# Respreading small VectorE work in a one-core retention, routing and two-layer expert kernel: decoding, slot positions, gates and one copy move

## Chip, core and metric

The kernel runs on one core of a Trainium2 chip. The metric is device time in microseconds (us) of one launch. Engines are named as the profile names them: PE is TensorE (its weight loads are PEld), DVE is VectorE, ACT is ScalarE, POOL is GpSimd, SP is the engine that issues most transfers.

## What is computed

The reference, cut to what matters:

```
def reference(q, k, v, moe_*, moe2_*):          # float32
    # 1. retention with decay: 4 batches, 8 heads, 576 positions, 64 wide
    scores = (q @ k.T) / 8
    ret = scores * gamma[h] ** (i - j) * (i >= j)
    x = (ret @ v).transpose(0, 2, 1, 3).reshape(2304, 512)
    # 2. router: 8 experts, top 1, one gate per token
    logits = normed(x) @ normed(expert_emb).T / tau
    e = argmax(logits);  gate = softmax(logits)[e]
    x[t] = gate[t] * (relu(x[t] @ w1[e]) @ w2[e])    # 512 -> 1024 -> 512
    # 3. dense layer on all tokens
    h = x @ w_in                                     # 512 -> 2048
    return elu(h) @ w_out                            # 2048 -> 512
```

## The kernel before

Products are made from float32 values split into a high and a low part (`split_of` on ACT makes the high part `ha`/`hb`, `split_low` on DVE the low part `la`/`lb`). The order of the program on each engine is the order of the Python code: nothing is scheduled by cost, and an engine that waits at one instruction holds back all that stands behind it on the same engine. SP likewise issues transfers in program order, on one queue. There are four stretches.

**Retention, 0 to 107 us.** Ten units (`UNITS`, u = 0 to 9) of up to 256 positions. `scale(u)` copies q into the layout that TensorE transposes (L289) and multiplies k by its decay (L282); unit 0 by DVE, all others by POOL. `transposes`, `scores`, `carried`, `values`, `summed` and `xrows` are TensorE's work of a unit, with ACT or DVE taking each result out of PSUM; the mask multiplication of `scores` (L339, tile `A`) is DVE's. Token tiles 0 to 17 are routed in four groups (0 to 4, 5 to 9, 10 to 12, 13 to 17). The small steps of a group (`expert_steps`, `gate_steps`) are generators that `pump` runs between the large instructions. The group of tiles 10 to 12 is the third one, index 2; its last steps, the gates (L570 to L578), run before the mask multiplication of the last unit, u = 9.

**End of the router, 107 to 124 us.** The last group's experts and gates (`ge`, `gg`), the order of the experts by their load (`go`, `order_steps`: tiles `key`, `gtm`, `pe`, `perm`, `pif`, `cnp`, `pi`, and then `pick`, which makes `idsp`, the row numbers of experts 1 to 7), the row numbers and gates of the first expert (`finish`: `ids0`, `gsl0`), and then the gather of the first expert's rows by POOL (L912), their multiplication by the gates (L921, L923), transposes (`xpose`) and the first products. `gather_expert(1)`, the gather of the second expert's rows, needs `idsp`.

**Experts, 120 to 357 us.** A loop over i = 0 to 64, eight steps for each of the eight experts, in the order that the router found. Step i makes `mm1(i)` (the products of the first layer, tile `h`), `mm2(i - 1)` (those of the second layer, tiles `acc`; its last four need `hl`), takes `h` out as `hh` (ACT) and `hl` (DVE, L976), splits one weight tile, loads the weight tile after next, and runs pieces of two other jobs. The first is decoding: the dense layer's weights arrive as 8-byte words and are rebuilt to float32 on DVE, 32 tiles (`draw` in, `wd` out), four DVE instructions each (L151, L153, L156, L159) and one of ACT (L154); `decode(n)` runs n of the four pieces. The last piece (L159) also has SP issue the load of the tile after next and the store of this one. The second is the table that maps output rows back to tokens (`compact`, then 18 times `compact_part`, at the steps in `WHEN`). At i = 48 (`IOVER`) stands a conditional, `overflow`, whose body is not run with these inputs; behind it the rows `yb` of the expert layer, four transfers of 384 KB (L1168, at i = 49 to 52), are loaded for the dense layer, and their sums (L1179, tiles T3, T2, T1, T4) are made by DVE at i = 54 and 55.

**Dense layer, 357 to 738 us.** TensorE with few gaps; the sums, splits and activations are on DVE, ACT and POOL.

Lines that the change and the steps of the prediction touch: `scale` L274 to L293; the pump behind `xrows` L745; the router's end L863 to L870; `compact` L1011 to L1031; the table of the first steps `WHEN` L1195; the decoding at L1306 to L1309; `sums` L1172.

Of the kernel before, what the change touches and what calls it, by code (L numbers as in the profile page):

```python
# [9 lines left out]
F32 = mybir.dt.float32  # L10
# [74 lines left out]
def tile_kernel(ctx: ExitStack, tc: tile.TileContext, q, k, v, emb, tau, w1, w2, w_in, w_out, const, out):  # L85
# [80 lines left out]
    def decode(n):  # L166
        for _ in range(n):
            next(dsteps, None)
# [105 lines left out]
    def scale(u):  # L274
        if u >= NU:
            return
        c = UNITS[u][1]
        scaled[u] = {nm: a2.tile([P, 2, H, D], F32, tag=nm + "s", name=f"{nm}s{u}") for nm in "qk"}
        eng = vec if u == 0 else pool

        def decayed(nm, s_, g_):
            eng.tensor_tensor(out=scaled[u][nm][:, s_], in0=loaded[u][nm][:, :, s_, :],  # L282
                              in1=C("g" + nm)[:, g_ * H:(g_ + 1) * H].unsqueeze(2).to_broadcast([P, H, D]), op=ALU.mult)

        m = len(slots_of(u))
        if u == NU - 1:
            decayed("q", 0, 4)
        else:
            eng.tensor_copy(out=scaled[u]["q"][:, :m].rearrange("p s h d -> p h s d"), in_=loaded[u]["q"][:, :, :m, :])  # L289
        if u == 0:  # L290
            meanwhile()
        for s_ in slots_of(u):
            decayed("k", s_, 2 * c + s_ if c >= 0 else 4)  # L293

    tT = {}
    copied = {}
# [355 lines left out]
    transposes(0, 1, "k")  # L652
    load(1, "v", copied[0, 1, "k"])
    scores(0, 0)
    pe = ps.tile([P, 2, 512], F32, tag="X", name="pemb")[:, 0, :2 * KD * NE].rearrange("p (b k e) -> p b k e", b=2, k=KD)
    for b, src in enumerate((e1, swap.rearrange("e k j d -> e (k j d)"))):
        for kk in range(KD):
# [4 lines left out]
            nc.scalar.copy(out=rhsx[b][o:o + 64, :, j, D:], in_=pe[o:o + 64, b])  # L662
    summed(0)
    transposes(1, 0, "q")
    load(2, "q", copied[1, 0, "q"])

    NG = len(GROUPS)
# [31 lines left out]
    for u in range(NU):  # L699
        ns = UNITS[u][2]  # L700
        before = UNITS[u - 1][2][1] if u and len(UNITS[u - 1][2]) > 1 else None
        if u == 1:
            load(3, "k")
        carried(u)
        scores(u, 1 if UNITS[u][1] >= 0 else 0)
        transposes(u + 1, 0, "qk" if u else "k")
        if u == 0:
            load(2, "k", copied[1, 0, "k"])
            nc.sync.dma_start(out=ct[:, gcols:], in_=const[:, gcols:CSMALL])
            nc.sync.dma_start(out=big[0][:, 2 * P:], in_=const[:, CSMALL + 2 * P:])  # L710
        else:
            load(u + 2, "v", copied.get((u + 1, 0, "k")))
        if held is not None:
            grouped(held)
        if before is not None:
            xrows(before)
        if u < NU - 1:
            pump(24, 0)
        summed(u + 1)
        scale(u + 2)  # L720
        if u == 0:
            pool.tensor_scalar(out=pre[:, 0, :], in0=C("base"), scalar1=1.0 / P, scalar2=None, op0=ALU.mult)
            pool.tensor_copy(out=lowb, in_=C("lower"))
            pool.tensor_copy(out=parts[:, :, :2], in_=C("id").rearrange("p (n two) -> p n two", two=2))
        if u == 7:
            load_a(0)
            load_b(0)
            load_a(1)
        transposes(u + 1, 1)
        load(u + 3 if u else 2, "q" if u else "v", copied.get((u + 1, 1, "k")))  # L730
        if u == NU - 2:
            decode_load(0)
            decode_load(1)
        values(u)
        load(u + 3, "k" if u else "q", copied[u, "x"])
        if before is not None:
            grouped(before)
        if u == NU - 1:
            while live:
                pump(100, 0)  # L740
        if u + 1 < NU and UNITS[u + 1][1] >= 0:
            scores(u + 1, 0)
        xrows(ns[0])
        held = ns[0]
        if u < NU - 1:  # L745
            pump(24, 0)
        for _ in range(6 if u > 6 else 4):
            if ready:
                slots(*ready.pop(0))
# [115 lines left out]
    begin(pig, 2, NPART)  # L865
    warm(8)
    next(fi)
    next(fi, None)
    for _ in interleave(gg, go):
        pass  # L870
    for _ in finish(pig, 2, NPART, gsl, gsl0):
        pass
# [130 lines left out]
        return lambda: eng.value_load(ap, min_val=0, max_val=top)  # L1003

    gather_expert(0)
    pool.memset(ord_["off"][:, 0:1], 0.0)
    for e in range(NE):
        pool.tensor_tensor(out=ord_["off"][:, e + 1:e + 2], in0=ord_["off"][:, e:e + 1], in1=ord_["cnp"][:, e:e + 1], op=ALU.add)
    pool.tensor_copy(out=offi, in_=ord_["off"][:, :NE])

    def compact():  # L1011

        oe = qp.tile([P, NE], F32, name="oe")
        vec.tensor_tensor(out=ord_["t"], in0=ord_["perm"].rearrange("q p e -> q e p"),
                          in1=ord_["off"][:, :NE].unsqueeze(1).to_broadcast([P, NE, NE]), op=ALU.mult)
        vec.tensor_reduce(out=oe, in_=ord_["t"], axis=AX.X, op=ALU.add)
        t = qp.tile([P, NT, NE], F32, name="po1")
        pos = qp.tile([P, NT], F32, name="pos")
        pool.tensor_tensor(out=oe, in0=oe, in1=C("base"), op=ALU.subtract)
        rf = qp.tile([P, NT], F32, name="rf")  # L1020
        pool.tensor_copy(out=rf, in_=rk)
        pool.tensor_tensor(out=t, in0=oh, in1=oe.unsqueeze(1).to_broadcast([P, NT, NE]), op=ALU.mult)
        vec.tensor_reduce(out=pos, in_=t, axis=AX.X, op=ALU.add)
        pool.tensor_tensor(out=pos, in0=pos, in1=rf, op=ALU.add)
        posi = qp.tile([P, 2, NT], I32, name="posi")
        posf = qp.tile([P, 2, NT], F32, name="posf")
        pool.tensor_copy(out=posi[:, 0, :], in_=pos)
        vec.tensor_scalar(out=posi[:, 1, :], in0=posi[:, 0, :], scalar1=127, scalar2=None, op0=ALU.bitwise_and)
        vec.tensor_scalar(out=posi[:, 0, :], in0=posi[:, 0, :], scalar1=7, scalar2=None, op0=ALU.arith_shift_right)
        pool.tensor_copy(out=posf, in_=posi)  # L1030
        return posf  # L1031

    cparts = {}

    def compact_part(n, posf):
        bt = qp.tile([P, P], BF16, name=f"cb{n}")
        at = qp.tile([P, NPART, NT], BF16, name=f"ca{n}")
        o18 = qp.tile([P, NT], BF16, name=f"co{n}", tag="co", bufs=2)
# [153 lines left out]

    QL = 3 * NQ
    MORE = {*range(1, 9), *range(10, 26, 3)}
    WHEN = [i for i in range(10, 38) if i % 8 in (1, 2, 4, 5, 6)]  # L1195
    slots_a = {"A11": 0, "A12": 1, "A22": 2, "S3": 3}
    slots_s = {"S1": 0, "S2": 1, "S4": 2}
    qra, qrs, qrb, qa, qs, qb = {}, {}, {}, {}, {}, {}
# [48 lines left out]
        low()  # L1247
    load_b(1, nc.scalar)
    load_a(2, nc.scalar)
    split_b(0)  # L1250
    for i in range(NI1 + 1):
        if i == IOVER - 1:
# [13 lines left out]
        if i == 0:  # L1266
            for _ in pick(gslp, gsl):
                pass
            gather_expert(1)
        e, f = divmod(i, 8)  # L1270
        if i < NI1:
            if f == 0 and e:
# [3 lines left out]
            if 3 <= f < 6 and e + 1 < NE:  # L1276
                weighs[e + 1](f - 3)
        if i == 9:
            posf = compact()
        if i in WHEN:  # L1280
            compact_part(WHEN.index(i), posf)
        if i == 41:
            compact_sum()
        if i == 42:
# [20 lines left out]
            low_(0, i - IOVER - 8)  # L1305
        elif i < IOVER - 1:  # L1306
            decode(3 if i in MORE else 2)
        elif IOVER < i < IOVER + 4:
            decode(3)  # L1309
        if i == NI1 - 3:  # L1310
            Sa(0)
        if i == NI1 - 2:
# [200 lines left out]
```

## Time and profile before

| | |
|---|---|
| median of 3 runs | 739.19 us (739.15 to 739.63) |
| the profiled execution's own time | 739.86 us |
| its span, first to last instruction | 738.0 us |
| PE busy | 711.1 us (96%) |
| DVE busy | 586.2 us (79%) |
| ACT busy | 447.5 us (61%) |
| POOL busy | 252.4 us (34%) |
| mean granted TensorE clock | 0.989 |

Busy time is the union of the instructions' records. Matmuls overlap in the pipeline and their ends are modelled, so the wait that a row of TensorE names is a little less than the time lost; where the same step recurs, the distance from one step's first product to the next one's tells the loss.

### The profile page before, as it was taken

How to read it: one execution, taken by the hardware profiler on the slowest of the kernel's cores; microseconds unless marked ns; L12 is line 12 of the kernel's file. 1: busy time of each engine (PE TensorE's matmuls, PEld its weight loads, DVE VectorE, ACT ScalarE, POOL GpSimd, SP SyncE). 2: the span in 40 equal slices, each digit the busy share in tenths (PEclk: the TensorE clock that was granted, in tenths of full speed). 3: DMA queues.
4: the chain of work that ended last, by engine and by line, in shares of the span. 5: the costliest groups of instructions: out<-in, count | busy, mean ns of one | idle time of the engine just before them, and what ended most of it. 6: DMA issues, size and time to landing. Idle time of an engine off the chain costs nothing.

```text
span 738.0 us, 15524 instructions
## 1 busy us (share of the span) xinstructions
PE 711.1 (96%) x5940; PEld 656.2 (89%) x5940; DVE 586.2 (79%) x940; ACT 447.5 (61%) x690; POOL 252.4 (34%) x347
## 2 busy tenths in 40 slices
PE   8999968999999999979999999999999999999996
PEld 6988866999999999979988999989999988989995
DVE  4566777889888898749799999987778997777773
ACT  3443443556656566547677677786665877656562
POOL 3436364127573661001522432264112237211103
PEclk9999998999999999989999999999999999999999
DMA  7777555899999989687434222235222124211012
GB/s 214 227 216 216 155 180 173 285 307 301 333 296 336 317 278 307 224 289 222 126 128 118 97 74 84 58 128 186 61 82 58 59 74 155 86 58 58 29 29 85
DMA packets 101987, 123.79 MB, mean 168 GB/s; under 512 B 12266, under 2 KB 72078, under 8 KB 101910
## 3 DMA queue, kind: packets, MB, share of 16 engines
q1 hardware_dynamic: 97622, 111.71, 48.0%
q0 software_dynamic: 3104, 9.83, 3.7%
q10 hardware_dynamic: 1184, 1.24, 0.6%
q8 instruction: 47, 0.77, 0.4%
q14 instruction: 30, 0.25, 0.1%
HBM read 99.91 MB, written 22.85 MB: 166 GB/s over the span
## 4 chain that ended last, share of the span: by engine, by line
issue 27%; PE 15%; POOL 9%; DVE 4%; ACT 2%; DMA 1%; SPq 0%; POOLq 0%; ACTq 0%
PE o L230 4%; PE X L230 3%; PE h L230 3%; PE Y L230 2%; POOL out_dram L1425 2%; POOL qs L1221 2%; POOL qs L1219 2%; POOL qs L1222 2%; POOL qa L1220 2%; PE acc L993 2%; DMA draw<-in_moe_w_in_dram 1%; PE acc L995 1%; DVE hB L1389 0%; DVE glA L1397 0%; DVE xB L1386 0%
## 5 line engine op out<-in xcount | busy, mean ns | idle before, releaser
L1219 POOL TENSOR_TENSOR qs<-qa 128x256 f32<-128x256 f32 x24 | 23.4, 973 | 250.1 <-DMA qa<-wd 52.5
L230 PE MATMUL h<-xth,ha 128*128 128x332 f32 (+7 forms) x252 | 75.1, 314 | 0.1
L993 PE MATMUL acc<-hh,lb 128*128 128x342 f32 (+7 forms) x256 | 73.8, 304 | 0.5 <-DVE lb L204 0.5
L993 PE MATMUL acc<-hh,hb 128*128 128x342 f32 (+7 forms) x256 | 73.7, 304 | 0.0
L230 PE MATMUL h<-xtl,ha 128*128 128x332 f32 (+7 forms) x252 | 72.9, 305 | 0.0
L1376 ACT ACTIVATE rA<-hA 128x768 f32<-128x768 f32 x24 | 20.4, 848 | 54.1 <-DVE hA L1369 54.1
L995 PE MATMUL acc<-hl,hb 128*128 128x342 f32 (+7 forms) x256 | 47.2, 307 | 5.5 <-DVE hl L976 5.4
L1361 DVE TENSOR_TENSOR u<-Y,m 128x384 f32<-128x384 f32 x48 | 26.6, 554 | 30.3 <-PE Y L230 28.3
L993 PEld LDWEIGHTS acc<-hh,lb 128*128 128x128 f32 x256 | 48.4, 189 | 1.0 <-DVE lb L204 1.0
L230 PEld LDWEIGHTS h<-xth,ha 128*128 128x128 f32 x252 | 48.1, 191 | 0.6 <-issue 0.3
L993 PEld LDWEIGHTS acc<-hh,hb 128*128 128x128 f32 x256 | 48.5, 189 | 0.0
L912 POOL DMA_INDIRECT row<-xd,idsp x21 | 24.3, 1158 | 70.7 <-ACT xth L953 61.9
L230 PEld LDWEIGHTS h<-xtl,ha 128*128 128x128 f32 x252 | 48.1, 191 | 0.0
L204 DVE TENSOR_TENSOR la<-ra,ha 128x1024 fp32r<-128x1024 f32 x32 | 39.3, 1230 | 9.9 <-ACT ha L199 9.8
L230 PE MATMUL h<-xth,la 128*128 128x332 f32 (+7 forms) x252 | 46.1, 305 | 0.0
L995 PEld LDWEIGHTS acc<-hl,hb 128*128 128x128 f32 x256 | 39.4, 190 | 6.2 <-DVE hl L976 6.2
L204 DVE TENSOR_TENSOR lb<-rb,hb 128x1024 fp32r<-128x1024 f32 x32 | 39.4, 1230 | 6.8 <-ACT hb L199 6.4
L1425 POOL DMA_INDIRECT out_dram<-ob,idc x18 | 20.3, 1126 | 68.4 <-ACT ob L1422 65.9
L154 ACT ACTIVATE dsq<-draw 128x512 f32<-128x512 f32 x32 | 21.8, 680 | 34.5 <-DVE db L159 10.5
L975 ACT ACTIVATE hh<-h 128x342 fp32r<-128x342 f32 (+7 forms) x64 | 27.2, 424 | 23.9 <-PE h L230 22.3
L230 PEld LDWEIGHTS h<-xth,la 128*128 128x128 f32 x252 | 39.0, 191 | 0.0
L339 DVE TENSOR_TENSOR A<-sc,ctbig 128x512 f32<-128x512 f32 (+1 forms) x36 | 22.1, 655 | 21.2 <-PE sc L334 21.2
(1690 smaller groups left out, 2328.8 us busy)
## 6 DMA issues: line engine op xcount, KB each, us to landing
ra<-in_moe_w_dram SPq DMA_DIRECT2D x31, 512.0 KB
rb<-in_moe_w_dram SPq DMA_DIRECT2D x31, 512.0 KB
qb<-wd SPq DMA_DIRECT2D x48, 256.0 KB
draw<-in_moe_w_in_dram SPq DMA_DIRECT2D x16, 512.0 KB
draw<-in_moe_w_out_dram SPq DMA_DIRECT2D x16, 512.0 KB
wd<-db SPq DMA_DIRECT2D x32, 256.0 KB
qa<-wd SPq DMA_DIRECT2D x24, 256.0 KB
qa<-wd SPq DMA_DIRECT2D x48, 128.0 KB
```

What stands on the lines that cost most here:

```text
L154: nc.scalar.activation(out=sq, in_=hw.bitcast(F32), func=AF.Square)
L204: nc.vector.tensor_tensor(out=lo, in0=src, in1=hi.bitcast(F32), op=ALU.subtract)
L230: nc.tensor.matmul(o, l, r, start=first and n_ == 0, stop=last and n_ == len(seq) - 1, skip_group_check=True)
L339: vec.tensor_tensor(out=t[:, :, :w], in0=sc[j][:, :, :w], in1=m.unsqueeze(1).to_broadcast([P, 4, w]), op=ALU.mult)
L912: pool.indirect_dma_start(out=t[:m].rearrange("p k w -> p (k w)"), out_offset=None, in_=xd[:, :], in_offset=bass.IndirectOffsetOnAxis(ap=i ...
L975: nc.scalar.activation(out=hh, in_=hp[:, :c], func=AF.Relu)
L993: nc.tensor.matmul(acc[d][:, :c], w[d][w_], hh, start=f == 0 and w_ == 0, stop=False)
L995: nc.tensor.matmul(acc[d][:, :c], w[d][0], hl, start=False, stop=f == 7)
L1219: pool.tensor_tensor(out=S1, in0=A21, in1=A22, op=ALU.add)
L1361: vec.tensor_tensor(out=S_[nm], in0=S_["Y"], in1=S_["m1"], op=ALU.add)
L1376: nc.scalar.activation(out=Q[n]["r" + z], in_=Q[n]["h" + z], func=AF.Relu, scale=-1.0)
L1425: ins = pool.indirect_dma_start(out=out[:, :], out_offset=bass.IndirectOffsetOnAxis(ap=idc[:, col:col + 1], axis=0), in_=ob, in_offset=None)
```

## The change

Five edits:

- **Second q by VectorE.** POOL no longer copies q of unit 1. DVE does, in two halves (`ordered(1, 0)` and `ordered(1, 1)`), each in front of the transposes that read it or well before.
- **Third group's gates.** The pump behind `xrows` in unit 8 runs one step in place of 24, so the gates of group 2 run after the last unit's `values` have been issued.
- **Router's end.** The last group's gates run without the order steps between them. The order steps and `idsp` run behind the first expert's transposes, in front of `split_b(0)`. The eight running sums of `off` (POOL) run behind `gather_expert(1)`.
- **Positions.** `compact` becomes a generator that runs over i = 9, 10 and 11; `WHEN` begins at 12 in place of 10 and ends one step later.
- **Decoding.** Behind the conditional nine pieces run as 3, 2, 0, 2, 2 at i = 49 to 53 in place of 3, 3, 3 at i = 49 to 51.

```
@@ scale
         if u == NU - 1:
             decayed("q", 0, 4)
-        else:
+        elif u != 1:
             eng.tensor_copy(out=scaled[u]["q"][:, :m].rearrange("p s h d -> p h s d"), in_=loaded[u]["q"][:, :, :m, :])
...
+    def ordered(u, s_):
+        vec.tensor_copy(out=scaled[u]["q"][:, s_], in_=loaded[u]["q"][:, :, s_, :])
@@ before the loop over units
     scores(0, 0)
+    ordered(1, 0)
...
     summed(0)
     transposes(1, 0, "q")
+    ordered(1, 1)
@@ loop over units, behind xrows(ns[0])
-            pump(24, 0)
+            pump(1 if u == NU - 2 else 24, 0)
@@ router's end
     next(fi)
+    while next(gg) != STEP:
+        pass
+    next(gg)
     next(fi, None)
-    for _ in interleave(gg, go):
+    for _ in gg:
         pass
@@ behind gather_expert(0): the running sums become a function, offsets(), called behind gather_expert(1)
@@ compact: three yields, the POOL and DVE instructions as before
-        return posf
+        cparts["pos"] = posf
+        yield
@@ tables
-    WHEN = [i for i in range(10, 38) if i % 8 in (1, 2, 4, 5, 6)]
+    REST = {IOVER + 1: 3, IOVER + 2: 2, IOVER + 4: 2, IOVER + 5: 2}
+    WHEN = [i for i in range(12, 39) if i % 8 in (1, 2, 4, 5, 6)]
@@ in front of the loop over i
     load_a(2, nc.scalar)
+    for _ in go:
+        pass
     split_b(0)
@@ in the loop over i
             gather_expert(1)
+            offsets()
...
-            posf = compact()
+            where_ = compact()
+        if 9 <= i < 12:
+            next(where_)
...
-        elif IOVER < i < IOVER + 4:
-            decode(3)
+        elif i in REST:
+            decode(REST[i])
```

How the rows move on DVE, at three places. A name ends in the number of its step, tile or unit and a number of the buffer; line numbers from L289 on are 3 to 17 higher in the changed kernel.

Behind the conditional, DVE, from the second product part of i = 51 on, before:

```order
L976 SCALAR_TENSOR_TENSOR hl51_6044<-h51_6030,hh51_6043 128x282
L204 TENSOR_TENSOR lb26_6061<-rb26_5427,hb26_6060 128x1024
L156 SCALAR_TENSOR_TENSOR db128_6026<-draw28_5377,db128_6026 128x512
L159 SCALAR_TENSOR_TENSOR db128_6026<-dsq28_6025,db128_6026 128x512
L151 TENSOR_SCALAR db129_6082<-draw29_6022 128x512
L976 SCALAR_TENSOR_TENSOR hl52_6098<-h52_6084,hh52_6097 128x282
```

And the same stretch of the changed kernel, up to the sums of `yb` that open the dense layer's operands:

```order
L204 TENSOR_TENSOR lb26_6060<-rb26_5428,hb26_6059 128x1024
L984 SCALAR_TENSOR_TENSOR hl52_6089<-h52_6075,hh52_6088 128x282
L962 TENSOR_TENSOR xtl_7_6105<-tp7_0_6106,xth_7_6104 128x4x128
L204 TENSOR_TENSOR la27_6115<-ra27_5919,ha27_6114 128x1024
L153 SCALAR_TENSOR_TENSOR db128_6027<-draw28_5378,db128_6027 128x512
L156 SCALAR_TENSOR_TENSOR db128_6027<-draw28_5378,db128_6027 128x512
L984 SCALAR_TENSOR_TENSOR hl53_6147<-h53_6133,hh53_6146 128x282
L962 TENSOR_TENSOR xtl_7_6105<-tp7_1_6162,xth_7_6104 128x4x128
L204 TENSOR_TENSOR lb27_6171<-rb27_5967,hb27_6170 128x1024
L159 SCALAR_TENSOR_TENSOR db128_6027<-dsq28_6026,db128_6027 128x512
L151 TENSOR_SCALAR db129_6190<-draw29_6023 128x512
L984 SCALAR_TENSOR_TENSOR hl54_6206<-h54_6192,hh54_6205 128x282
```

The first piece of tile 29 (L151, which reads `draw29`) stood in front of `hl52` and now stands in front of `hl54`. Behind `hl54` both programs have the last transposed part, then `la28`, then the first sum of `yb` (T3, which needs all four transfers). On SP's queue the load of `draw30` and a store of `wd`, which L159 of tile 28 issues, stood in front of the load of `ra29` and the last `yb` transfer, and now stand behind them and the load of `rb29`.

In the last units of the retention, DVE, before (`A00_9` and `A10_9` are the masks of the last unit, `gate2` the third group's gates):

```order
L442 TENSOR_REDUCE lg3_2012<-lh15_2199 128x8
L570 TENSOR_REDUCE gate2_2031<-ex2_2030 128x3
L572 TENSOR_SCALAR gate2_2031<-gate2_2031 128x3
L574 RECIPROCAL gate2_2031<-gate2_2031 128x3
L578 CAST parts_75<-gate2_2031 128x3
L581 TENSOR_TENSOR gate2_2031<-gate2_2031,parts_75 128x3
L339 TENSOR_TENSOR A00_9_2259<-sc0_9_0_2241,ctbig_135 128x4x64
```

And of the changed kernel:

```order
L445 TENSOR_REDUCE lg3_2013<-lh15_2200 128x8
L342 TENSOR_TENSOR A00_9_2252<-sc0_9_0_2234,ctbig_135 128x4x64
L342 TENSOR_TENSOR A10_9_2254<-sc1_9_0_2235,ctbig_135 128x4x64
L442 TENSOR_TENSOR xs16_2263<-xa16_2258,ct_67 128x512
L444 TENSOR_TENSOR lh16_2265<-xa16_2258,ct_67 128x64
L445 TENSOR_REDUCE lg3_2013<-lh16_2265 128x8
L573 TENSOR_REDUCE gate2_2032<-ex2_2031 128x3
```

Eight gate steps (of which the first rows show five) moved from in front of the masks to behind tile 16's results, in front of tile 17's `lg`.

At the router's end, DVE, the place to which the order steps moved, of the changed kernel (before, `lb0` stands directly behind the `xtl` row):

```order
L962 TENSOR_TENSOR xtl_0_2478<-tp0_2_2495,xth_0_2477 128x4x86
L793 SCALAR_TENSOR_TENSOR key_2387<-cn_2386,ct_67 128x8
L795 SCALAR_TENSOR_TENSOR key_2387<-ohf_79,key_2387 128x8
L797 TENSOR_TENSOR gtm_2388<-key_2387 128x64
L799 TENSOR_REDUCE pe_2389<-gtm_2388 128x8
L801 TENSOR_TENSOR perm_2390<-pe_2389,ct_67 128x64
L807 TENSOR_REDUCE cnp_2532<-gtm_2388 128x8
L809 CAST pi_83<-pif_2531 1x8
L818 TENSOR_TENSOR pick_2539<-perm_2390,ids_76 128x192
L822 TENSOR_REDUCE idsp_81<-pick_2539 128x24
L204 TENSOR_TENSOR lb0_2543<-rb0_1927,hb0_2542 128x1024
```

Twelve rows in all moved there (nine are shown); before, they stood one by one between the last group's gate steps.

## Rows read from the trace of the kernel before

**Rows 1.** Page, part 1: busy time, share, instructions.

```profile
PE 711.1 (96%) x5940; PEld 656.2 (89%) x5940; DVE 586.2 (79%) x940; ACT 447.5 (61%) x690; POOL 252.4 (34%) x347
```

**Rows 2.** Windows by TensorE's steps: length, busy of five engines, PEclk, DMA share, GB/s.

```profile
309.78:313.28 3.50, 3.50 (x31) 3.50 (x29) 2.36 (x4) 1.80 (x3) 0.00 (x0) 1.00 0.79 262
313.28:322.88 9.60, 4.68 (x31) 4.43 (x30) 3.13 (x6) 2.45 (x4) 0.00 (x0) 0.82 1.02 359
322.88:328.02 5.14, 5.14 (x30) 4.95 (x28) 2.50 (x4) 2.54 (x4) 0.00 (x0) 0.68 0.85 278
331.28:334.40 3.12, 3.12 (x26) 3.12 (x25) 3.08 (x5) 0.58 (x2) 0.00 (x0) 1.00 0.50 168
```

**Rows 3.** Timeline behind the conditional: start, us, engine, line, operation [idle before, releaser].

```profile
320.23 0.43 DVE L151 TENSOR_SCALAR db<-draw 128x512 int32<-128x512 int32 x1 [6.47 <-DMA draw<-in_moe_w_in_dram]
321.07 1.31 PE L995 MATMUL acc<-hl,hb 128*128 128x282 f32 x4 [4.92 <-DVE hl L976]
323.21 0.51 SPq L1168 DMA_DIRECT2D yb<-yd  x1
...
330.48 0.95 DVE L1179 TENSOR_TENSOR yb<-yb 128x768 f32<-128x768 f32 x1
...
332.34 0.45 DVE L976 SCALAR_TENSOR_TENSOR hl<-h,hh 128x282 fp32r<-128x282 f32 x1
```

**Rows 4.** Two windows of DMA traffic behind the conditional; columns as in rows 2.

```profile
316.00:324.00 8.00, 3.08 (x15) 2.92 (x14) 2.99 (x6) 0.74 (x3) 0.00 (x0) 0.71 1.04 379
325.00:328.00 3.00, 3.00 (x21) 2.83 (x20) 1.59 (x2) 0.81 (x2) 0.00 (x0) 0.80 0.83 263
```

**Rows 5.** Timeline of the first units, q and k of unit 1.

```profile
5.35 0.69 DVE L289 COPY qs<-q 128x1024 f32<-128x1024 f32 x1 [5.35 <-DMA q<-in_q_dram]
...
11.72 1.04 POOL L289 COPY qs<-q 128x1024 f32<-128x1024 f32 x1 [7.55 <-DMA q<-in_q_dram]
13.24 2.04 POOL L282 TENSOR_TENSOR ks<-k,ct 128x512 f32<-128x512 f32 x2 [0.48 <-DMA k<-in_k_dram]
...
12.81 0.66 PE L309 MATMUL qTp<-ident,qs 128*128 128x128 f32 x4 [0.90 <-POOL qs L289]
```

**Rows 6.** Timeline of the last unit of the retention.

```profile
100.62 0.17 DVE L570 TENSOR_REDUCE gate<-ex 128x3 f32<-128x24 f32 x1
...
102.20 0.17 DVE L578 CAST parts<-gate 128x3 bf16<-128x3 f32 x1
...
105.76 0.23 DVE L434 TENSOR_REDUCE lg<-xa 128x8 f32<-128x64 f32 x1 [1.70 <-PE xa L427]
...
102.75 1.02 PE L372 MATMUL xTp<-A,v 64*64 64x64 f32 x32 [0.95 <-DVE A L339]
```

**Rows 7.** Windows of TensorE's steps i = 9 and i = 11; columns as in rows 2.

```profile
153.97:157.60 3.63, 3.63 (x26) 3.63 (x25) 3.50 (x7) 2.39 (x6) 0.00 (x0) 1.00 0.96 300
161.31:166.19 4.88, 4.20 (x26) 3.66 (x25) 4.21 (x8) 0.74 (x2) 3.88 (x7) 1.00 0.85 288
```

**Rows 8.** Timeline of the router's end and the first expert's start.

```profile
111.10 0.13 DVE L788 SCALAR_TENSOR_TENSOR key<-cn,ct 128x8 f32<-128x8 f32 x1
...
114.08 0.35 DVE L817 TENSOR_REDUCE idsp<-pick 128x24 int32<-128x192 f32 x1
...
116.29 0.72 ACT L923 ACTIVATE row<-row,gsl 128x512 f32<-128x512 f32 x1 [4.60 <-DMA row<-xd,ids]
...
117.20 1.44 PE L948 MATMUL tp<-ident,row 128*128 128x128 f32 x8
...
123.31 1.22 DVE L204 TENSOR_TENSOR lb<-rb,hb 128x1024 fp32r<-128x1024 f32 x1 [2.28 <-ACT hb L199]
```

**Rows 9.** Timeline of the second expert's gather, its first issue and first use.

```profile
118.82 1.00 POOL L912 DMA_INDIRECT row<-xd,idsp  x1 [0.40 <-issue]
...
132.69 0.71 ACT L923 ACTIVATE row<-row,gslp 128x512 f32<-128x512 f32 x1
```

**Rows 10.** POOL's `cb` instructions by shape: least/median/most ns, from when to when.

```profile
L1039 POOL TENSOR_SCALAR cb<-ct,posf x18: 595/602/2776, 163.8 to 259.2; 128x128 bf16<-128x128 f32 x18
```

More of the change, by code (lines that the diff above doesn't have):

```diff
@@ L1005, in tile_kernel, with offsets @@
     gather_expert(0)
[L1006 to L1009, printed above, removed]
+    def offsets():
+        off, cnp = ord_["off"], ord_["cnp"]
+        pool.memset(off[:, 0:1], 0.0)
+        for e in range(NE):
+            pool.tensor_tensor(out=off[:, e + 1:e + 2], in0=off[:, e:e + 1], in1=cnp[:, e:e + 1], op=ALU.add)
+        pool.tensor_copy(out=offi, in_=off[:, :NE])
     def compact():
@@ L1018, in compact @@
         pos = qp.tile([P, NT], F32, name="pos")
+        rf = qp.tile([P, NT], F32, name="rf")
+        posi = qp.tile([P, 2, NT], I32, name="posi")
+        posf = qp.tile([P, 2, NT], F32, name="posf")
         pool.tensor_tensor(out=oe, in0=oe, in1=C("base"), op=ALU.subtract)
-        rf = qp.tile([P, NT], F32, name="rf")
         pool.tensor_copy(out=rf, in_=rk)
         pool.tensor_tensor(out=t, in0=oh, in1=oe.unsqueeze(1).to_broadcast([P, NT, NE]), op=ALU.mult)
+        yield
         vec.tensor_reduce(out=pos, in_=t, axis=AX.X, op=ALU.add)
         pool.tensor_tensor(out=pos, in0=pos, in1=rf, op=ALU.add)
-        posi = qp.tile([P, 2, NT], I32, name="posi")
-        posf = qp.tile([P, 2, NT], F32, name="posf")
         pool.tensor_copy(out=posi[:, 0, :], in_=pos)
+        yield
         vec.tensor_scalar(out=posi[:, 1, :], in0=posi[:, 0, :], scalar1=127, scalar2=None, op0=ALU.bitwise_and)
@@ L1030, in compact, with compact_part @@
         pool.tensor_copy(out=posf, in_=posi)
-        return posf
+        cparts["pos"] = posf
+        yield
     cparts = {}
-    def compact_part(n, posf):
+    def compact_part(n):
+        posf = cparts["pos"]
         bt = qp.tile([P, P], BF16, name=f"cb{n}")
@@ L1278, in tile_kernel @@
         if i == 9:
-            posf = compact()
+            where_ = compact()
+        if 9 <= i < 12:
+            next(where_)
         if i in WHEN:
-            compact_part(WHEN.index(i), posf)
+            compact_part(WHEN.index(i))
         if i == 41:
```

## The prediction

> **What bounds it now.** The page's busy times come first: PE works in 96% of the span [rows 1], so an edit can only pay where PE stands still or runs at a lower clock. The list of PE's waits gives the places, and one is far larger than the rest: 4.92 us for `hl` behind the conditional [rows 3]. The chain that ended last is mostly PE's own work and names no other engine for a long piece, so I read the stretches where PE waits, one by one: a timeline of each, and windows cut at the starts of PE's steps, which tell what a step costs beside its neighbours. PE's work is unchanged; whatever brings PE forward at one place carries through to the end, as long as nothing that it meets later becomes late. Each term below is therefore a shift of PE.
>
> **Unit 1's q.** PE's transposes start at 12.81 after a wait for POOL's copy, which began when q landed, at 11.72, and took 1.04; DVE copied a whole q of that size in 0.69 [rows 5]. The half that DVE now copies lies between 0.35 (half of that) and 0.69; I take 0.40, since a fixed part of each instruction doesn't halve. PE starts at 11.72 + 0.40 + 0.03 = 12.15: **0.65 gained** (0.35 to 0.70). The next thing that could be late is POOL's decay of k, whose two halves end at 15.28 [rows 5] and wait for k, not for POOL; half of it is done by 14.26, and PE, earlier by 0.65, uses that half about 14.65. The Trainium skill speaks against this edit: "SBUF — State Buffer", section "Who interferes with whom", says that a VectorE copy can take a port pair that GpSimd needs, as an exclusive lock for a whole instruction. By that rule the second half copy would hold POOL's multiplication by up to 0.40, and this term would be some 0.6 instead of 0.65; no row of before shows such a pair side by side.
>
> **Third group's gates.** Eight gate steps stand on DVE from 100.62 to 102.37, ahead of the last unit's masks; PE waits 0.95 for the mask, up to 102.75 [rows 6]. With them gone the masks start 1.75 earlier by DVE's queue, but the scores they read set them next; PE's wait is what can be had, and with the pipeline's start 0.1 more: **1.05 gained** (0.5 to 1.3). The steps go to where DVE stood idle for 1.70 ahead of the last tile's `lg` [rows 6]; without that cover they would cost their 1.75 there.
>
> **Router's end.** The twelve order steps span 3.33 on DVE, from 111.10 to 114.43 [rows 8], with gate steps between them; alone they take somewhat less, I take 3.0 (2.8 to 3.33). Taking them out lets the gates end about 1 us earlier. Most of that is lost at once: ACT's weighing at 116.29 waits for the gathered rows, not for gates [rows 8]. What stays is the part of the eight transposes at 117.20 (1.44 in all, [rows 8]) that belongs to the first row tile, weighed by DVE: half of it, 0.7, can be done while PE waits for the second. So the first expert's last `xtl` ends 0.7 earlier, at 123.31 - 2.28 - 0.7 = 120.33. There the steps now stand in front of `lb0`: 120.33 + 3.0 = 123.33, and `lb0` started at 123.31. The 2.28 of idle time ahead of `lb0` [rows 8] is the cover, and it is just used up: **0** (from +0.4 to -1.05, the latter if nothing is earlier and the steps take 3.33).
>
> **Second expert's gather.** Its issue at 118.82 moves to the end of the order steps, about 123.4, ahead of the `off` sums, which nothing needs for long. The first use, ACT at 132.69, named no wait [rows 9]: 9.3 us from issue to use remain, where three issues take about 1 us each. **0.**
>
> **Positions.** The step i = 11 took 4.88 where i = 9 took 3.63; POOL was busy 3.88 in it with the positions [rows 7], and DVE's share of them stood ahead of `lb` and `hl`. Spread over three steps, POOL's 3.88 and DVE's share are smaller than a step's slack each: **1.2 gained** (0.9 to 1.25).
>
> **Decoding behind the conditional.** DVE's L151 of tile 29 waits 6.47 for `draw29`, landing at 320.2, and holds `hl52` behind it, which PE waits for until 321.07 [rows 3]. By the windows of PE's steps, i = 52 took 3.50; 53 took 9.60 and 54 took 5.14 at granted clocks of 0.82 and 0.68; 56 took 3.12 [rows 2]. For 54, with half the transposes of 52, I take 3.3 as its time at full clock. The loss is 9.60 + 5.14 - 3.50 - 3.3 = 7.9, of which 4.9 is the wait and 3.0 the time at 1.2 in place of 2.4 GHz that followed PE's standstill. In the changed order L151 stands in front of `hl54`, two steps later; steps 53 and 54 at 3.50 and 3.3 bring DVE there at about 321, after the landing. So this wait goes.
>
> What is late next is the sum T3 of `yb`, which needs the last `yb` transfer and stands ahead of `hl55`. Step 56 would start at 313.28 + 3.50 + 3.3 + 3.12 = 323.20, and want `hl55` for its last four products (0.65 at full clock, 1.31 at half, [rows 3]) at 323.20 + 3.12 - 0.65 = 325.67. From the start of T3 to the end of `hl55` it was 330.48 to 332.79, 2.31 [rows 3]. T3 must start by 323.36. On SP's queue the last `yb` issue was at 323.21 [rows 3], held by the load of `ra29`, whose buffer DVE frees with `la27`; in the changed kernel it is free some 5 us earlier, and the data move behind those of `draw29`: `wd` 256 KB, `rb28` 512, `yb` 384, `ra29` 512 and `yb` 384 (by their shapes in float32), 2048 KB or 2.10 MB. At the 379 GB/s of the window 316 to 324 [rows 4] that takes 5.5 us behind 320.2: T3 at 325.8, and PE waits 325.8 - 323.36 = 2.4 in step 56. At the 263 GB/s of 325 to 328 [rows 4] it is 328.2 and 4.8. The queue is full in this stretch, so I take 379. A standstill half as long as before I take to leave the clock alone. **7.9 - 2.4 = 5.5 gained.**
>
> **Sum.** 0.65 + 1.05 + 0 + 0 + 1.2 + 5.5 = 8.4. The profiled execution's own time is 739.86 (span 738.0 and 1.9 around it); 739.86 - 8.4 = 731.5. The median of the three runs, 739.19, is 0.67 below it, so 730.8.
>
> **Rivals.**
> - *The new wait costs the clock too.* For it: the wait of before brought 1.2 GHz for most of steps 53 and 54 [rows 2], and a later `yb` makes the new one as long. Against: at 379 GB/s it is half as long. 730.8 + 3.0 = 733.8; with the data at 328.2, 2.4 more, 736.2.
> - *No wait left.* The last `yb` would have to land by 323.36, 2.10 MB in 3.1 us, 670 GB/s, against 379 as the fastest of [rows 4], unless less is queued ahead than I count. 730.8 - 2.4 = 728.4.
> - *The order steps show ahead of `lb0`.* For it: cover and steps are equal to 0.02 in my sum. If the transposes are no earlier, 1.05 of PE's time: 731.9.
> - *Slower: the second expert's rows come late.* The gather starts 4.6 later and now runs beside DVE's wide splits. A POOL instruction beside DVE can take 2776 ns where 602 is the middle [rows 10]; three issues and their descriptors so stretched eat the 9.3 us of cover. Past that, PE loses one for one, and the kernel is slower than before if the rows land later than 9.3 + 8.4 = 17.7 us after the issue, 19.2 for a loss of 0.2%: 740.9 or more. Before, they were there at the latest 13.9 after it (118.82 to 132.69, [rows 9]). The section of the skill named above would make this mechanism the port lock, with GpSimd writing the descriptors of such a transfer; rows 9 and 10 alone don't tell the cause of the 2776 ns.
>
> **Numbers.** The forecast has 0.58, its own range 729.5 to 732.3 (the wait between 1.5 and 3.3, the small terms by their bounds). The longer wait or the clock 0.22, no wait 0.08, order steps 0.09, late rows 0.03. The range 728.3 to 735.0 holds all but the last and the worst third of the second. A change of 0.2%, 1.5 us, is what this kernel's times can tell from none: every case but the late rows is well beyond it; 0.03 stays for a mixture that ends inside. Faster 0.94, same 0.03, slower 0.03.
>
> **What would show it.** In the profile of the changed kernel: the first transposes of unit 1 near 12.15, named after DVE; no wait for the mask of the last unit; `lb0` at about the distance from the first expert's products that it had; step i = 11 at 3.6 to 3.8; no wait of L151 behind the conditional; T3 as the DVE instruction that waits for DMA, and one PE wait of about 2.4 for `hl` three steps later than before, with a granted clock near 1.00. I am wrong if the clock halves there again, if PE doesn't wait there at all, or if a wait for `xth` or `row` appears at the second expert.

## The result: 6.7 us faster

The changed kernel takes 732.73 us (median of 6 runs, 732.27 to 735.86) where the kernel before takes 739.41 (6 runs, 739.05 to 740.9): a ratio of 0.9915, 95% interval 0.9896 to 0.9935. The forecast was 730.8, its range 728.3 to 735.0. The profiled execution took 732.69, with a span of 730.9 where before it was 738.0: 7.1 us to be accounted for, against 8.4 forecast.

The page of the changed kernel, part 1, to be read beside [rows 1]:

```profile
PE 707.7 (97%) x5939; PEld 653.5 (89%) x5940; DVE 587.9 (80%) x942; ACT 447.2 (61%) x690; POOL 253.4 (35%) x346
```

Windows of the changed kernel. The first four are PE's steps i = 1, 10, 11 and 18, the next five its steps 53 to 57 [rows 2, 7]; the last line is those five together:

```profile
117.33:124.14 6.81, 6.03 (x37) 5.75 (x38) 6.47 (x19) 4.19 (x6) 1.94 (x2) 1.00 0.64 164
155.32:159.81 4.49, 3.94 (x27) 3.67 (x25) 4.42 (x8) 3.00 (x5) 0.93 (x1) 1.00 1.05 326
159.81:163.49 3.68, 3.68 (x27) 3.68 (x26) 3.65 (x7) 0.25 (x2) 2.43 (x4) 1.00 1.04 381
186.59:190.43 3.84, 3.72 (x27) 3.46 (x25) 3.81 (x6) 2.44 (x4) 2.35 (x3) 1.00 0.95 310
311.24:314.83 3.59, 3.59 (x31) 3.59 (x30) 1.82 (x2) 3.02 (x5) 0.00 (x0) 1.00 1.02 338
314.83:318.52 3.69, 3.69 (x32) 3.50 (x30) 3.59 (x7) 2.44 (x4) 0.00 (x0) 1.00 1.05 388
318.52:321.80 3.28, 3.28 (x27) 3.28 (x25) 2.57 (x5) 2.52 (x4) 0.00 (x0) 1.00 1.06 382
321.80:327.19 5.39, 3.39 (x27) 3.17 (x26) 2.97 (x4) 0.60 (x2) 0.00 (x0) 1.00 0.92 343
327.19:330.38 3.19, 3.19 (x26) 3.09 (x25) 3.19 (x5) 3.19 (x8) 0.00 (x0) 1.00 0.39 148
...
311.24:330.38 19.14, 17.14 (x131) 16.63 (x130) 14.14 (x20) 11.77 (x22) 0.00 (x0) 1.00 0.90 325
```

The same windows of the kernel before, where its rows did not stand yet (i = 1, i = 18, and the five steps 53 to 57 together):

```profile
120.12:126.42 6.30, 6.02 (x36) 5.74 (x37) 3.99 (x7) 3.25 (x5) 1.85 (x2) 1.00 0.83 247
189.29:192.74 3.45, 3.45 (x26) 3.45 (x25) 3.42 (x6) 1.99 (x3) 3.37 (x4) 1.00 1.07 331
...
313.28:337.49 24.21, 19.29 (x132) 18.86 (x131) 13.53 (x19) 11.18 (x21) 0.00 (x0) 0.86 0.80 271
```

Behind the conditional the five steps fell from 24.21 to 19.14 us: 5.1 of the 7.1. The granted clock is 1.00 throughout; 5.39 in step 56 shows that one wait is left. Steps i = 10 and i = 18 are longer than before (3.71 and 3.45), which no edit meant.

The timeline of the changed kernel behind the conditional, to be read beside [rows 3]:

```profile
315.38 0.50 SPq L1183 DMA_DIRECT2D yb<-yd  x1
...
319.03 0.42 DVE L151 TENSOR_SCALAR db<-draw 128x512 int32<-128x512 int32 x1
...
324.18 0.96 DVE L1194 TENSOR_TENSOR yb<-yb 128x768 f32<-128x768 f32 x1 [3.09 <-DMA yb<-yd]
...
326.55 0.80 PE L1003 MATMUL acc<-hl,hb 128*128 128x282 f32 x4 [2.00 <-DVE hl L984]
```

L151 of tile 29 no longer waits. The last `yb` transfer is issued 7.8 us earlier than before, lands at 324.18, and the sum T3, with `hl55` and PE behind it, is what waits.

The first units and the last one of the retention [rows 5, 6], and the start of the first expert [rows 8], in the timeline of the changed kernel:

```profile
7.70 1.29 DVE L282 TENSOR_TENSOR ks<-k,ct 128x512 f32<-128x512 f32 x2 [1.53 <-DMA k<-in_k_dram]
...
12.31 0.43 DVE L296 COPY qs<-q 128x512 f32<-128x512 f32 x1
...
12.79 0.66 PE L312 MATMUL qTp<-ident,qs 128*128 128x128 f32 x4 [0.19 <-DVE qs L296]
...
100.95 0.69 PE L375 MATMUL xTp<-A,v 64*64 64x64 f32 x32
...
121.03 1.22 DVE L204 TENSOR_TENSOR lb<-rb,hb 128x1024 fp32r<-128x1024 f32 x1
...
122.30 0.42 PE L1001 MATMUL acc<-hh,lb 128*128 128x342 f32 x1 [0.78 <-DVE lb L204]
```

The mask's wait of 0.95 is gone. Unit 1's transposes start at 12.79, not near 12.15 as the prediction named. `lb0` stands directly behind the order steps, with no idle time of DVE, and PE's wait for it is 0.78, where before it was 0.28:

```profile
124.59 0.43 PE L993 MATMUL acc<-hh,lb 128*128 128x342 f32 x1 [0.28 <-DVE lb L204]
```

So the first expert step is 0.5 longer than before (6.81 against 6.30).

ACT in the changed kernel at the steps around i = 9, and PE's first wait there:

```profile
151.53 0.69 ACT L154 ACTIVATE dsq<-draw 128x512 f32<-128x512 f32 x1 [3.68 <-DMA draw<-in_moe_w_in_dram]
...
157.87 0.42 PE L1001 MATMUL acc<-hh,hb 128*128 128x332 f32 x1 [0.55 <-ACT hh L983]
```

The same `dsq` in the kernel before, and the load that it reads, in the kernel before and in the changed one:

```profile
153.03 0.68 ACT L154 ACTIVATE dsq<-draw 128x512 f32<-128x512 f32 x1 [2.87 <-DVE hl L976]
147.40 0.37 SPq L137 DMA_DIRECT2D draw<-in_moe_w_in_dram  x1
...
145.11 0.37 SPq L137 DMA_DIRECT2D draw<-in_moe_w_in_dram  x1
```

PE is 2.3 us earlier here than before (step i = 9 begins at 151.69 in place of 153.97, as the starts of PE's products show), and so is the issue of the load. But the load landed only 1.5 earlier: from its issue to `dsq` it is 6.4 us in place of 5.6. `hh`, the next result that PE needs, stands behind `dsq` on ACT.

### The profile page after: what moved, and what is told of

Same layout as the page of the kernel before. It is cut to its first block, busy times and chain, and to the rows that moved or that the text cites. A ratio compares the mean times of both kernels' runs of the same rounds, so it can differ in the third digit from the quotient of the medians.

```text
span 730.9 us, 15524 instructions
## 1 busy us (share of the span) xinstructions
PE 707.7 (97%) x5939; PEld 653.5 (89%) x5940; DVE 587.9 (80%) x942; ACT 447.2 (61%) x690; POOL 253.4 (35%) x346
## 3 DMA queue, kind: packets, MB, share of 16 engines
q10 hardware_dynamic: 1184, 1.24, 0.6%
## 4 chain that ended last, share of the span: by engine, by line
issue 22%; PE 21%; POOL 7%; DVE 5%; ACT 2%; DMA 2%; POOLq 0%; SPq 0%; ACTq 0%; DVEq 0%
PE o L230 8%; PE X L230 5%; PE Y L230 4%; PE h L230 2%; PE acc L1001 2%; POOL out_dram L1446 1%; POOL qs L1238 1%; POOL qs L1235 1%; POOL qs L1237 1%; DMA yb<-yd 1%; POOL qa L1236 1%; PE acc L1003 1%; DVE hB L1410 0%; DVE glA L1418 0%; DVE xB L1407 0%
```

## Experiments

In each part "before" is the kernel before and "changed" the changed kernel; every ratio is to the kernel before, timed on the same chip.

**1. Respreading alone**, on before:

```
+    REST = {IOVER + 1: 3, IOVER + 2: 2, IOVER + 4: 2, IOVER + 5: 2}
-        elif IOVER < i < IOVER + 4:
-            decode(3)
+        elif i in REST:
+            decode(REST[i])
```

> The kernel before with the decoding respread alone (3, 2, 0, 2, 2 pieces). My theory: the wait of 6.5 us for draw29 goes, the sum T3 waits for the last yb transfer instead, PE waits about 2 us in step 56 at full clock; the five steps 53 to 57 take about 19.2 us in place of 24.2, so the kernel gains about 5.0 us (734.3). Rival: the new wait halves TensorE's clock again in most executions, the gain is 2 us (737.3) and the granted clock falls behind step 56. Rival: the gain of the full change there needs the earlier PE of the other edits; then T3 waits for nothing and the gain is over 7.

Measured: 735.32 us (7 runs, 734.18 to 736.14), ratio 0.9935 (0.9912 to 0.9958). Windows of its steps 56 and 57, and the sum in its timeline:

```profile
323.80:328.62 4.82, 3.38 (x26) 3.15 (x25) 2.96 (x4) 0.59 (x2) 0.00 (x0) 1.00 0.90 337
328.62:331.84 3.22, 3.22 (x26) 3.12 (x25) 3.22 (x5) 3.22 (x8) 0.00 (x0) 1.00 0.48 149
```
```profile
325.63 0.96 DVE L1179 TENSOR_TENSOR yb<-yb 128x768 f32<-128x768 f32 x1 [2.54 <-DMA yb<-yd]
```

The five steps take 18.6 us, 5.6 less than before; the wait for `yb` takes the place of that for `draw29`, at full clock. The theory holds in this execution, whose span is 5.7 us shorter than before; it is the fastest of the seven, and by the medians 4.2 us arrive. In three of the seven the mean granted clock was 0.991, at 735.3 to 736.1 us, in the other four 0.994 to 0.997, at 734.2 to 735.5. Whether the new wait lowered the clock in those three, as the first rival has it, stays open: they have no trace.

**2 and 3. Which transfer is waited for.** Changed, with the sums one step later, and changed, with the four `yb` transfers in two steps:

```
-        if i in (IOVER + 6, IOVER + 7):
+        if i in (IOVER + 7, IOVER + 8):
...
-        elif IOVER + 8 <= i < IOVER + 15:
+        if IOVER + 8 <= i < IOVER + 15:
```

> The changed kernel with the four sums of yb one step later (i = 55 and 56 in place of 54 and 55), transfers as they are. My theory: the wait that is left is T3's for the last yb transfer, which landed at 324.18 while hl was wanted at 324.4; one step later the data are there, PE's wait of 2.0 us in step 56 goes and the kernel gains 2.0 to 2.3 us against the changed kernel (730.5). Rival: all of the stretch is short of transfers, and a weight tile or another transfer waits in place of yb: gain under 1 us.

```
-        if IOVER < i <= IOVER + KD:
-            LY(0, [i - IOVER - 1])
+        if IOVER < i <= IOVER + KD // 2:
+            LY(0, [2 * (i - IOVER) - 2, 2 * (i - IOVER) - 1])
```

> The changed kernel with the four yb transfers issued two by two at i = 49 and 50 in place of one each at 49 to 52. My theory: the last yb lands before ra29, draw29 and rb28, some 4 us earlier, T3 waits for nothing, gain 2.0 to 2.3 us (730.5). Rival: what is moved back (draw29 for L151, rb28 and ra29 for lb28 and la29) is late in its turn, and a wait of 1 to 5 us for it takes the place: 731 to 736.

Sums later: 731.5 us (4 runs, 731.02 to 732.44), ratio 0.988 (0.9841 to 0.992). Windows of its steps 56 and 58:

```profile
322.49:325.61 3.12, 3.12 (x27) 3.12 (x26) 2.26 (x3) 0.60 (x2) 0.00 (x0) 1.00 1.04 399
...
328.68:332.54 3.86, 3.34 (x27) 3.12 (x25) 3.86 (x6) 3.74 (x5) 0.00 (x0) 1.00 0.90 268
```

Step 56 falls from 5.39 to 3.12, as the theory says; step 58 rises to 3.86, because the sums now stand beside the first splits of the dense layer's operands. So of the 2.0 to 2.3 us expected 1.2 arrive by the medians. `yb` transfers early: 730.82 (4 runs, 729.79 to 731.77), ratio 0.9875 (0.9835 to 0.9915). Its step 56 and DVE there:

```profile
320.75:324.25 3.50, 3.39 (x27) 3.16 (x26) 3.47 (x5) 1.65 (x3) 0.00 (x0) 1.00 1.04 393
```
```profile
319.27 0.43 DVE L151 TENSOR_SCALAR db<-draw 128x512 int32<-128x512 int32 x1 [1.24 <-DMA draw<-in_moe_w_in_dram]
...
321.26 0.95 DVE L1194 TENSOR_TENSOR yb<-yb 128x768 f32<-128x768 f32 x1
```

T3 waits for nothing, and step 56 is 1.9 shorter; `draw29`, moved back, is late by 1.24, of which 0.4 reaches PE. The theory holds, and the rival takes 0.4 of its 2.3.

**4. Positions alone**, on before (`compact` as a generator with its three yields, and):

```
-            posf = compact()
+            where_ = compact()
+        if 9 <= i < 12:
+            next(where_)
```

> The kernel before with the positions alone spread over i = 9, 10 and 11. In the changed kernel the step i = 11 fell from 4.88 to 3.68, but i = 10 rose from 3.71 to 4.49. Theory A (a loaded weight word tile, draw, landed only 1.5 us earlier while PE came 2.3 us earlier, so transfers took 0.78 back): alone, with PE not earlier, i = 10 stays at 3.71 and i = 11 falls to 3.7, a gain of 1.2 there, of which some 0.6 may be lost at i = 18 and at the conditional, 738.1 to 738.7. Theory B (the first third of the positions itself lengthens i = 10): i = 10 is 4.5 here too and the gain is 0.4, 738.9.

Measured: 739.33 us (10 runs, 738.45 to 741.43), ratio 0.9991 (0.9974 to 1.0007): nothing. Windows of its steps i = 10, 11 and 18, and ACT at two places:

```profile
157.20:161.38 4.18, 3.93 (x26) 3.66 (x25) 4.05 (x8) 2.98 (x5) 0.91 (x1) 1.00 1.07 312
161.38:165.02 3.64, 3.64 (x27) 3.64 (x25) 3.61 (x7) 0.77 (x2) 2.38 (x4) 1.00 1.02 391
188.41:192.55 4.14, 3.93 (x27) 3.56 (x25) 4.11 (x6) 2.58 (x5) 1.31 (x2) 1.00 0.87 267
```
```profile
153.12 0.69 ACT L154 ACTIVATE dsq<-draw 128x512 f32<-128x512 f32 x1 [3.37 <-DMA draw<-in_moe_w_in_dram]
...
185.05 0.70 ACT L154 ACTIVATE dsq<-draw 128x512 f32<-128x512 f32 x1 [4.07 <-DMA draw<-in_moe_w_out_dram]
```

The step with the positions falls by 1.24, from 4.88 to 3.64, but i = 10 and i = 18, ahead of which `dsq` waits for a `draw` transfer, are longer by 0.47 and 0.69. Neither theory is right as written: what the edit saves it saves, but i = 10 grew although PE was only 0.4 earlier.

**5 to 7. The router's end, the gates, and q, each alone**, on before. Of the router's end all three places of the change (gates, order steps, `offsets`), of q `scale` and the two calls of `ordered`; their core:

```
+    for _ in go:
+        pass
     split_b(0)
```
```
-            pump(24, 0)
+            pump(1 if u == NU - 2 else 24, 0)
```
```
-        else:
+        elif u != 1:
             eng.tensor_copy(out=scaled[u]["q"][:, :m].rearrange("p s h d -> p h s d"), in_=loaded[u]["q"][:, :, :m, :])
```

> The kernel before with the router's end alone changed (gates without the order steps between them, order steps behind the first expert's transposes). In the changed kernel TensorE's first expert step began 1.0 us earlier than the step before would make it, and was 0.5 longer (6.80 in place of 6.30), with 0.8 of waiting for lb0. Theory: the same here, 0.5 us gained at the second step; then the draw transfer at i = 10, whose landing already set ACT's dsq in the kernel before, takes most of it back: 738.9 to 739.4. Rival (the prediction's sum): cover and steps cancel, no gain at the second step. Rival: the gain stays, 738.8 or less, with i = 10 at 3.71.

> The kernel before with the third group's gates alone moved. Theory: TensorE is 1.05 us earlier behind the last unit's masks and keeps that to the first experts; at i = 10 ACT waits for the draw transfer, and i = 10 becomes some 0.4 to 0.8 longer than 3.71, so 0.3 to 0.6 us are left: 738.8. Rival (the prediction's sum): 1.05 carries through, i = 10 stays at 3.7, 738.2.

> The kernel before with unit 1's q copied by VectorE alone. Theory: the transposes of unit 1 start 0.65 us earlier relative to the steps ahead of them; of this the draw transfer at i = 10 takes some back, and the whole kernel shows 0 to 0.6 us, inside what can be told (738.8 to 739.4). Rival (the rule of the shared port): POOL's decay of k is held by the second half copy and its two halves take clearly more than 2.04 us.

| alone | us, median (range, runs) | ratio (95% interval) |
|---|---|---|
| router's end | 739.6 (738.38 to 741.51, 10) | 1.0002 (0.999 to 1.0015) |
| gates | 738.41 (736.95 to 740.17, 10) | 0.9991 (0.9978 to 1.0004) |
| q | 738.53 (737.03 to 742.51, 10) | 0.999 (0.997 to 1.001) |

None can be told from no change by its time; their traces say more. Router's end, DVE's order steps, first and last of twelve, and `lb0`:

```profile
120.51 0.16 DVE L788 SCALAR_TENSOR_TENSOR key<-cn,ct 128x8 f32<-128x8 f32 x1
...
123.10 0.35 DVE L817 TENSOR_REDUCE idsp<-pick 128x24 int32<-128x192 f32 x1
123.37 1.22 DVE L204 TENSOR_TENSOR lb<-rb,hb 128x1024 fp32r<-128x1024 f32 x1
```

They take 2.94 us, and `lb0` starts at 123.37 (before: 123.31): against the trace of before nothing is gained, as the prediction's sum had it and my theory of the experiment had not. But the trace of before is slow just there. From the start of PE's last four `warm` products, whose result nothing reads, to its first expert step, in the kernel before and in number 1, whose programs are equal in this stretch:

```profile
115.19:120.12 4.93, 4.29 (x24) 2.36 (x21) 3.91 (x9) 1.75 (x3) 3.69 (x10) 0.72 0.20 64
...
115.55:119.63 4.08, 3.08 (x24) 1.83 (x22) 3.84 (x9) 1.75 (x3) 3.14 (x10) 1.00 0.25 88
```

The granted clock was 0.72 in the one and 1.00 in the other. From PE's first product behind the last mask to step i = 2 it is 23.7 us in the trace of before, 22.5 to 22.8 in the five others that leave the router's end as it was (numbers 1, 4, 6, 7 and 10), 23.0 to 23.2 in the seven that change both it and the gates, and 23.6 here. The first expert step takes 6.8 to 6.9 us in all eight kernels with the edit and 6.3 in all six without. So the edit costs some 0.5 us.

Its step i = 10 is 4.28 long with PE no earlier than before, which again says that the transfer's landing, not PE's progress, is what varies there. With the gates alone PE starts behind the masks at 101.73, 1.02 earlier than before, and step i = 10 is 3.99, 0.3 longer (by then PE is 2.2 earlier, since before lost time at the router's end). With q alone PE's transposes start at 12.40, and POOL's decay beside DVE's second half copy:

```profile
13.24 0.41 DVE L296 COPY qs<-q 128x512 f32<-128x512 f32 x1
13.29 2.27 POOL L282 TENSOR_TENSOR ks<-k,ct 128x512 f32<-128x512 f32 x2 [9.11 <-DMA k<-in_k_dram]
```

2.27 in place of 2.04 [rows 5]: 0.23 more where the two start together (2.32 in number 10); in the changed kernel, where DVE's copy began 0.4 ahead and was nearly done, it was 2.04. Where POOL began 0.3 to 0.5 ahead (numbers 12 and 8), DVE's copy took 1.05 and 0.78 in place of 0.41. The trace agrees in kind with the Trainium skill, "SBUF — State Buffer", section "Who interferes with whom" (one of the two is held while the other has the shared ports). PE did not wait for it.

**8 and 9. The load of the tile after next one piece earlier** (behind the third piece, the last that reads `draw`), on the changed kernel, and together with the early `yb` transfers:

```
             nc.vector.scalar_tensor_tensor(out=b1, in0=lw, scalar=29, in1=b1, op0=ALU.logical_shift_right, op1=ALU.bitwise_or)
+            decode_load(i + 2)
             yield
...
-            decode_load(i + 2)
             nc.sync.dma_start(out=wd[m][f], in_=b1.bitcast(F32))
```

> The changed kernel with the load of the tile after next issued one piece earlier (behind the third piece, the last one that reads draw, in place of the fourth). Theory: ACT's dsq waits for draw at i = 10 and i = 18, and hh stands behind it on ACT; the load comes 1 to 2 us earlier, so i = 10 falls from 4.49 to about 3.7 and i = 18 from 3.84 to 3.45, gain 1.0 to 1.4 us against the changed kernel (731.5). Rival: the transfer queue is full, an earlier issue lands no earlier or makes a weight tile late by as much: i = 10 stays over 4.3 or another step grows, gain under 0.3.

> Both improvements together: the load of the tile after next one piece earlier, and the yb transfers two by two at i = 49 and 50. If the two waits are separate, the gains add: 1.9 us from yb (its profile had 0.4 of the wait left) and 1.0 to 1.4 from draw, 729.5 to 730. If both only shift the same full transfer queue, no better than yb alone (730.8).

Load earlier: 732.07 us (4 runs, 729.49 to 734.11), ratio 0.9887 (0.9855 to 0.9919). Windows of its steps i = 10 and 18, then 56 and 57:

```profile
155.79:159.45 3.66, 3.66 (x26) 3.66 (x25) 3.53 (x8) 3.12 (x5) 1.04 (x1) 1.00 0.95 298
...
186.19:189.64 3.45, 3.45 (x27) 3.45 (x26) 3.42 (x6) 1.99 (x3) 3.37 (x4) 1.00 0.97 308
...
320.60:327.08 6.48, 3.37 (x27) 3.15 (x25) 2.96 (x4) 1.59 (x3) 0.00 (x0) 1.00 0.96 356
327.08:331.65 4.57, 4.57 (x26) 4.57 (x25) 4.57 (x7) 4.57 (x9) 0.00 (x0) 0.63 0.64 190
```

The long steps are gone, 1.2 us, as the theory says. But PE now comes to step 56 earlier while `yb` lands when it did: PE waits 3.11 there and the granted clock is 0.63 in the step behind it, which is 1.4 longer than in the changed kernel:

```profile
324.09 0.96 DVE L1194 TENSOR_TENSOR yb<-yb 128x768 f32<-128x768 f32 x1 [4.18 <-DMA yb<-yd]
...
326.46 0.78 PE L1003 MATMUL acc<-hl,hb 128*128 128x282 f32 x4 [3.11 <-DVE hl L984]
```

This is the prediction's first rival, seen in the profile of a kernel that it was not written for, at a wait between the 2.00 that left the clock alone and the 4.92 of before. The profile is of the slowest of the four executions. Together with the early `yb`: 729.5 (4 runs, 729.0 to 730.21), ratio 0.9867 (0.9846 to 0.9888); step 56 is 3.13. As far as the intervals can tell, the gains add.

**10 to 12. What the other edits are worth in company.** Three parts taken back, each a part of the change's diff read from + to -: the router's end, from number 9, the best kernel so far; the decoding, from the changed kernel; the positions, from number 9.

> The best so far (changed kernel, load of the tile after next one piece earlier, yb two by two) with the router's end as before. Theory, from the run with the router's end alone, where the second step began within 0.05 us of before: no difference, 729.5. Rival: with the gates of the third group out of the way the order steps are hidden between the last gates and cost 0.5 in front of lb0, so the old order is better by 0.5 to 0.7, 728.9, and the first expert step is 6.3 in place of 6.8.

> The changed kernel with the decoding behind the conditional as before (3, 3, 3). Theory: the four other edits bring PE 2 us earlier into the conditional; the wait for draw29 is as before, so 737 to 737.5, and respreading is worth some 5 of the 6.7 us. Rival: the wait for draw29 takes the 2 us back because the transfer lands no earlier: 739.

> The best so far (changed kernel, load of the tile after next one piece earlier, yb two by two) with the positions in one step as before. Theory: the positions are worth their 1.2 us as soon as no draw transfer takes them back: i = 11 is 4.9 here, 730.7. Rival: what the positions save is lost again to transfers in later steps here too: 729.5.

| | us, median (range, runs) | ratio (95% interval) |
|---|---|---|
| best, router's end as before | 728.81 (727.89 to 729.88, 4) | 0.9855 (0.9828 to 0.9881) |
| changed, decoding as before | 736.78 (734.17 to 739.1, 9) | 0.9962 (0.9938 to 0.9986) |
| best, positions as before | 730.04 (729.76 to 730.62, 4) | 0.987 (0.9846 to 0.9893) |

The first expert step of the best kernel with the router's end as before:

```profile
116.89:123.20 6.31, 6.02 (x37) 5.74 (x37) 4.02 (x7) 4.19 (x6) 2.44 (x3) 1.00 0.77 248
```

6.31 in place of 6.81 (number 9): the rival, for the profile, and the comparison of all traces at numbers 5 to 7 says the same. By the medians, whose ranges touch, it is not settled. Without the positions' edit, i = 10 stays at 3.66 and i = 11 takes 4.74:

```profile
158.76:163.50 4.74, 4.17 (x26) 3.63 (x25) 4.07 (x8) 1.18 (x4) 3.87 (x7) 1.00 0.80 258
```

so the edit is worth 1.1 there, once the transfers don't take it. The medians of numbers 9 and 12, from different chips, differ by 0.5, which is less than they can tell. All edits but the decoding bring 2.0 us by the medians; the respreading, alone, 4.2. The sum of 6.2 is close to the 6.7 of all five.

## Why the prediction was right, and where it was off

The direction, the largest term and its mechanism held; the time came out 1.9 us above the forecast, inside the range. Of the smaller terms the gates came as forecast, the q and the router's end did not, and part of the positions' gain was lost again.

- *Unit 1's q: 0.65 forecast*, not shown. The transposes start at 12.79, before at 12.81. Ahead of the edit unit 0's k had landed at 7.70 in place of 7.00, where nothing is changed and PE's wait was between 0.4 and 1.9 in ten of the twelve experiments; without the edit such a delay is in part hidden by PE's wait for POOL (in number 4 `k` cost PE 0.97, and the transposes were 0.51 late). Over all traces the transposes start at 12.1 to 13.0 in the nine with the edit and at 12.7 to 13.3 in the five without it, 0.4 apart in the mean. POOL's decay beside DVE's copy cost PE nothing.
- *Gates: 1.05 forecast*, 1.02 in the run with it alone.
- *Router's end: 0 forecast; it costs some 0.5*, within the term's bounds. The order steps stand ahead of `lb0` as the sum had it. What failed is the 0.7 that was to pay for them: the first expert step begins 16.2 us behind the last mask's wait in numbers 6 and 10, without the edit, and 16.2 to 16.4 behind it in the seven kernels with it and the gates. The rows that the 0.7 was read from lie in the stretch where the trace of before ran at a granted clock of 0.72. This is the rival "the order steps show ahead of `lb0`" at half its price. That the span of the changed kernel still gains 0.48 here is owed to that slow stretch, which is luck.
- *Second expert's gather: 0 forecast*, and no wait of PE names its rows.
- *Positions: 1.2 forecast*, 4.88 to 3.68.
- *Conditional: 5.5 forecast, 5.1 measured.* The new wait was found where it was forecast: T3, behind the last `yb`, PE held in step 56. The step lost 2.26 to it (5.39 against 3.13; 2.4 forecast). The term was mis-sized in the normal lengths: without a wait step 53 takes 3.59 and step 54 takes 3.69, not the 3.50 and 3.3 of the sum. That the wait came out so close is in part luck: PE came to step 56 at 321.80 in place of 323.20, and `yb` landed at 324.18 in place of 325.8. In number 1, where PE comes to the conditional as before, T3 starts at 325.63 and step 56 takes 4.82: of what the other four edits brought PE forward, 0.6 was lost again in this wait.
- *What failed* is a step of the first paragraph, that PE's advance carries through "as long as nothing that it meets later becomes late". I took that as given, and ahead of the conditional 1.43 us were lost again: 0.78 at i = 10, 0.39 at i = 18, both with `dsq` waiting for a `draw` transfer, and 0.26 from 291 to 296 us, whose cause no run shows.
  - At i = 18 the loss comes with the positions' edit, which brings PE forward by 1.2 at i = 11. The step takes 3.45 in the five kernels without the positions' edit and with the load at its old place, 3.48 to 4.15 in the five that have the edit, and 3.45 again in the four with the load one piece earlier. The trace of before names this transfer: ACT waits 2.06 us for it.
  - At i = 10 it is the transfer's own spread. In the kernel before, that `dsq` began at 153.03 with DVE named as its releaser; its data had come just then. With the load at its old place the step takes 3.87 to 4.67 in nine kernels, and the length doesn't follow the advance: 4.28 with none (number 5), 3.96 with 2.5 us (number 3). The 3.71 of before is the shortest of the ten, and one trace of before could not tell so. The four kernels with the load one piece earlier have 3.66.
- Two gains of some 0.4 each lie in the retention, at 58 and 89 us, where no edit stands. The second appears in all kernels that have the q edit, the first in some; no run settles them.

The sum: 0.02 (k late, q) + 0.76 (retention) + 1.02 (gates) + 0.48 (router's end, in these two traces) + 1.20 (positions) - 1.43 + 5.07 (conditional) = 7.1 us, the difference of the spans.

The longest of the six runs, 735.86, had a mean granted clock of 0.987 where the others had 0.992 or 0.993. That fits the first rival, a wait in step 56 long enough to lower the clock; number 8's profile shows that it can happen, but this run has no trace, and a longer stretch of low clock at the router's end would fit as well.

## What to carry over

An engine that is moved forward meets the next thing that had no margin, and the trace of before need not name it: a wait is put down to whoever came last. So follow the moved engine through every transfer whose landing lies close to its use, not only the ones beside the edits. And one trace is one execution: at two places the trace of before was not the usual case, the shortest i = 10 of ten and a router's end at low clock. Before a term is read from a row, compare the row in several traces, and look at the clock of its stretch. When a full queue decides, what helps is the order and the moment of issue: a load issued right behind the last reader of its buffer, and the data of the next stage ahead of what is wanted later, gave 3.2 us here on top of the five edits, by the medians.

## Not expected of the hardware

- The lengths of PE's steps i = 2 to 9 agree within 0.03 us between all fourteen profiles, while the start of `dsq` that waits for the same `draw` load, taken from the start of step i = 9, differs by up to 1.0 us among the ten with the load at its old place: at these steps the spread lies in the transfers, not in PE's products.
- A PE wait of 2.00 us left the granted clock at 1.00 in the step behind it; one of 3.11 brought 0.63 there, and the step from 3.2 to 4.57 us.
- POOL's chain of eight one-element sums (`off`) took 3.24 us before and 4.99 in the changed kernel, where it runs beside DVE's weight splits.
